# A scan and gated-MLP kernel on one core: VectorE's hand-written order with two weight pieces in turn, and the ninth unit on split weights

## The chip, the cores and the metric

The kernel runs on one core of a Trainium2 chip. The metric is the device time of one execution in microseconds, as a median of several runs; lower is better.

## What is computed

The inputs are x (4 batches, 8 heads, 768 positions, 32 values), decays a, and the matrices B and C of a state of 16 values, with three weight matrices of a gated MLP. First a linear attention with decay is computed in chunks, then the MLP on its output, viewed as 3072 tokens of 256 values. The reference, cut to what matters:

```python
for c in range(nc):                                   # chunks of the sequence
    cum = np.cumsum(la, axis=-1)                      # la = log(clip(a, 1e-6, 1))
    L = np.exp(cum[:, :, :, None] - cum[:, :, None, :]) * causal
    M = np.einsum('bhin,bhjn->bhij', Cc, Bc) * L
    y_intra = np.einsum('bhij,bhjd->bhid', M, xc)
    y_inter = np.einsum('bhin,bhnd->bhid', Cc, state) * np.exp(cum)[:, :, :, None]
    y[:, :, sl] = y_intra + y_inter
    state = decay_full[:, :, None, None] * state + np.sum(Bx, axis=2)
g = x @ w_gate                                        # x: y as 3072 x 256; d_ff = 1536
out = (g / (1 + np.exp(-g)) * (x @ w_val)) @ w_out
```

## The kernel before

The sequence is cut into six blocks of 128 positions; a block holds 512 tokens of the four batches together. For each block the kernel scans the decays (L), makes scores (S), mixes them (M), sums states (st) and values (y), and hands x to the MLP. The MLP of a block has twelve units, one for each 128 columns of the 1536: unit f of block k makes a gate half (gv k f 0) and a value half (gv k f 1) in two PSUM banks, ScalarE makes the silu (si k f), VectorE the product (pr k f), and later the output sums (po) follow. Blocks 3 to 5 use a scheme with fewer multiplications, on weight sums that GpSimd makes.

fp32 precision is had in two ways. A whole unit multiplies fp32 weights by fp32 x (four passes a matmul). A split unit uses a high and a low part of both, in three products that run at the faster fp32r rate: xh and xl for x, wh and wl for weights, where the low part is what the rounded high part leaves. The weights come as 64-bit numbers and are converted on the chip, piece by piece (pieces 0 to 11 are the units, 12 to 17 the output weights): mag and rest on ScalarE, range on VectorE or GpSimd, then on VectorE shift, sign and round, each on the result of the one before (lines 704 to 714). round gives the whole weight; wh (ScalarE) and wl follow from it. The first WHOLE units of block 0 (line 1332: nine) run whole, since their high and low parts come later: for these pieces ScalarE writes the negated weight (minus, line 720) and GpSimd starts a DMA that adds the weight to wl (line 729); for later pieces VectorE subtracts (line 732). x's low part in block 0 is made in the same way, by two negated copies on ScalarE (minus x, line 606) and one adding DMA of GpSimd (line 609).

The order of the work is made by a planner when the kernel is built (class Plan, lines 49 to 195): each step has an engine, a cost, a rank, prerequisites and buffers, and the planner issues steps as they come free on its own clock. For the first 60 us the order is instead written out by hand, one list for each engine (FRONT, lines 1346 to 1375). An engine runs its list in this order; a step that waits holds up all behind it. Behind the lists the planner is free. FAR (line 1337) names the pieces whose range goes to GpSimd. PSUM has four banks for units (mm): a unit's half takes the bank of the half two units earlier, when si has read the gate half and pr the value half.

What the change touches: the four lists of FRONT for VectorE, ScalarE and GpSimd (TensorE's stays), w_low, the steps of x in block 0 (lines 1230 to 1234), WHOLE, MINUS, FAR, and the order of loads in SP's queue for the later blocks (line 1315).

Of the kernel before, what the change touches and what calls it, by code (L numbers as in the profile page):

```python
# [23 lines left out]
K = P // Q  # L24
# [192 lines left out]
def scan_moe_kernel(ctx: ExitStack, tc, aj, an, bc, xb, wgv, wo, cst, own, first_e, e_table, out):  # L217
# [387 lines left out]

    def first_minus(g):
        se.activation(xl[0][:, g], whole[0][:, g], AF.Copy, scale=-1.0)

    def first_low():
        ge.dma_start(xl[0], whole[0], accum_op=ALU.add)  # L610

# [431 lines left out]
    for i in range(NW):  # L1043
# [7 lines left out]
        e, c = ("Pool", 2.2) if far else ("DVE", 0.335)  # L1051
        add(e, c, do(w_range, i, ge if far else ve), r - 4.5, [("mag", i), *([("round", i - 1)] if i == 1 else [])], gives=("range", i))
        add("Act", 0.57, do(w_rest, i, "Act"), r - 4.5, [("raw", i), *([("xf", 5)] if i == 3 else [])], gives=("rest", i))
# [6 lines left out]
        n, c = (slice(2 * P, 4 * P), 0.35) if not i else (slice(0, 4 * P), 0.6)  # L1060
        add("DVE", 0.335 if i else 0.2, do(w_shift, i, n), r - 4.2, [("range", i), *gate], gives=("shift", i))
        add("DVE", c, do(w_sign, i, n), r - 3.9, [("shift", i), *gate], gives=("sign", i))
        add("DVE", c, do(w_round, i, n), r - 3.3, [("sign", i), ("rest", i)], uses=[("raw", i)], gives=("round", i))
# [76 lines left out]
    for k in range(NB):  # L1140
# [86 lines left out]
        if not k:  # L1227
            add("-", 0.0, new_whole, -9, [("clip", 1)], takes=[("xl", "xf")], gives="xf")
            add("-", 0.0, do(new_x, 0), due(0, WHOLE) - 9, [("xf", i) for i in range(6)], takes=[("xh", ("xh", 0)), ("xl", ("xl", 0))], gives=("x", 0))
            for g in range(2):  # L1230
                r = due(0, WHOLE) - 7 + 2 * g
                add("Act", 0.57, do(first_high, g, "Act"), r, [("x", 0)], gives=("xh", 0, g))
                add("Act", 0.57, do(first_minus, g), r + 0.5, [("x", 0), ("gv", 0, 4, 0)], gives=("minus", "x", g))
            add("Pool", 1.2, first_low, due(0, WHOLE) - 4.5, [("minus", "x", g) for g in range(2)], uses=["xf"], gives=("xl", 0, 0), lag=1.6)
            for n, i in enumerate(FIRST_X):
                add([("Act", 0.2 if i % 3 else 0.36)], None, do(x_whole, i), -1 + n / 10, [("y" if i % 3 else "vals", *((0,) if i % 3 else ()), i // 3), "xf"], uses=[y[i]], gives=("xf", i))
            continue
# [9 lines left out]
    for k in range(FAST):  # L1247
        xs = [(t, k, i) for t in ("xh", "xl") for i in range(2 * K if k else 2) if k or t == "xh" or not i]
        for f in range(NF):
# [63 lines left out]
    for steps in ORDER:  # L1313
        plan.follow(steps)
    for k in range(FAST + 1, NB):
        plan.follow([("aj", k), ("bc", k), ("E", k), ("xb", k)])
# [31 lines left out]
clip 0, clip 1, row, scan0 0, scan0 1, scan0 2, scan0 3, L 0 0, L 0 1, L 0 2, L 0 3, bt 0, M 0 0, M 0 1, ce 0, M 0 2, M 0 3,  # L1348
shift 0 gate, sign 0 gate, round 0 gate, shift 0, sign 0, round 0, range 1, shift 1, sign 1, round 1, range 2, products, shift 2, sign 2, round 2,
pr 0 0, shift 3, sign 3, round 3, pr 0 1, shift 4, sign 4, round 4, step 0 1, shift 5, pr 0 2, sign 5, round 5,  # L1350
shift 6, sign 6, round 6, pr 0 3, shift 7, sign 7, round 7, shift 8, sign 8, pr 0 4, round 8, L 1 0, L 1 1, L 1 2, pr 0 5,
L 1 3, shift 9, bt 1, sign 9, M 1 0, pr 0 6, M 1 1, M 1 2, M 1 3, round 9, pr 0 7, wl 9, shift 10, sign 10, round 10,
pr 0 8, wl 10, ce 1, step 1 0, shift 11, sign 11, round 11, pr 0 9, wl 11, pr 0 10, xh 1 0, xh 1 2, xl 1 0, xl 1 2, xl 1 1, xl 1 3,
step 1 1, shift 12, pr 0 11, sign 12, round 12, wl 12
# [87 lines left out]
```

## Time and profile before

| What | Before |
|---|---|
| Median of 3 runs | 339.32 us (338.32 to 340.19) |
| Profiled execution | 337.55 us, its span 335.8 us |
| TensorE busy (matmul) | 330.2 us, 98% of the span |
| VectorE, ScalarE, GpSimd busy | 70%, 52%, 54% |
| Mean granted clock of TensorE | 0.998 |

The span runs from the first to the last instruction of the profiled execution. All instructions of the kernel are recorded by one helper and so have one line (L206); they are told apart by the tiles they write and read. wg8w is the weight of piece 8 while it is converted, wg8h and wg8l its high and low part, sg a silu or product, T the states. A shift is a TENSOR_SCALAR on int32, a range one on f32, a sign a SCALAR_TENSOR_TENSOR, a round the CUSTOM instruction. Matmuls overlap one another, so a duration of one is longer than the distance to the next.

### The profile page before, as it was taken

To read this page: it belongs to the slowest core of one execution; us is meant where nothing else is said; L and a number is where in the kernel's file an instruction comes from. 1 tells how busy PE (TensorE), PEld (TensorE's weight loads), DVE (VectorE), ACT (ScalarE), POOL (GpSimd) and SP (SyncE) were. 2 spreads that over 40 slices of the span, in tenths; PEclk is the share of its full clock that TensorE was granted. 3 is DMA by queue.
4 is the path that set the end of the run, shared out by engine and by line. 5 is a ranking of instruction groups with operands and counts; after the bars stand their busy time and mean duration, and the time that the engine had idled before them with its cause. 6 is when DMAs were issued, how large, how long until landed. Compare 5 with 4: busy or idle time off the path is not lost.

```text
span 335.8 us, 8400 instructions
## 1 busy us (share of the span) xinstructions
PE 330.2 (98%) x3506; PEld 276.3 (82%) x3506; DVE 235.0 (70%) x411; ACT 175.0 (52%) x321; POOL 181.3 (54%) x164
## 2 busy tenths in 40 slices
PE   7999999999999999999999999999999999999996
PEld 6645757888888888878888999888999978999985
DVE  7899999878699981575199478843499934376600
ACT  5799957546245543545371686332575341656411
POOL 2378841511213109887979997450479560368460
PEclk9999999999999999999999999999999999999999
DMA  7899975990000761000091100008500000100001
GB/s 249 288 395 284 261 163 152 297 228 15 1 2 8 206 169 63 1 2 2 17 241 62 62 2 2 2 4 217 164 0 1 5 2 2 62 2 0 2 0 62
DMA packets 10100, 31.05 MB, mean 92 GB/s; under 512 B 1455, under 2 KB 2223, under 8 KB 9423
## 3 DMA queue, kind: packets, MB, share of 16 engines
q1 hardware_dynamic: 7192, 24.21, 23.7%
q0 software_dynamic: 1440, 2.88, 4.8%
q10 hardware_dynamic: 1431, 3.43, 3.5%
q8 instruction: 27, 0.44, 0.6%
q14 instruction: 10, 0.08, 0.1%
HBM read 24.29 MB, written 3.35 MB: 82 GB/s over the span
## 4 chain that ended last, share of the span: by engine, by line
PE 95%; DVE 2%; DMA 1%; issue 0%; SPq 0%; DVEq 0%
PE po L206 30%; PE gv L206 29%; PE pq L206 23%; PE y L206 5%; PE r L206 4%; PE S L206 2%; DVE L L206 1%; PE a L206 1%; DMA pick<-in_own 1%; DVE sg L206 0%; PE st L206 0%; DVE wg9w L206 0%; DVE wg8w L206 0%; PE rest L206 0%; DVE last L206 0%
## 5 line engine op out<-in xcount | busy, mean ns | idle before, releaser
L206 POOL TENSOR_TENSOR pl<-hp,ph 128x512 fp32r<-128x512 f32 x36 | 46.7, 1310 | 25.8 <-PE po L206 14.9
L206 POOL TENSOR_TENSOR sp<-sp 128x256 f32<-128x256 f32 x36 | 30.5, 848 | 32.0 <-ACT sp L206 29.9
L206 DVE TENSOR_TENSOR pq<-pq,sp 128x512 f32<-128x512 f32 x36 | 25.0, 694 | 14.4 <-PE pq L206 14.3
L206 ACT COPY sp<-pq 128x512 f32<-128x512 f32 x36 | 21.1, 587 | 20.2 <-PE pq L206 19.8
L206 ACT ACTIVATE sg<-gv 128x512 f32<-128x512 f32 x36 | 21.5, 597 | 17.6 <-PE gv L206 17.3
L206 DVE TENSOR_TENSOR_SCAN L<-L,dj 128x520 f32<-128x520 f32 x20 | 29.5, 1506 | 0.9 <-DMA L<-clipped 0.9
L206 DVE TENSOR_TENSOR sp<-r,sp 128x256 f32<-128x256 f32 x36 | 15.0, 418 | 20.4 <-POOL sp L206 20.4
L206 DVE TENSOR_TENSOR sg<-gv,sg 128x512 f32<-128x512 f32 x28 | 19.2, 684 | 11.5 <-PE gv L206 8.8
L206 ACT ACTIVATE hp<-pq 128x512 f32<-128x512 f32 x36 | 20.2, 602 | 11.0 <-DVE pq L206 9.6
L206 ACT CAST ph<-hp 128x1024 fp32r<-128x1024 f32 x18 | 18.8, 1052 | 13.1 <-PE po L206 7.9
L206 ACT COPY ob<-po 128x512 f32<-128x512 f32 x12 | 7.0, 587 | 35.4 <-PE po L206 34.9
L206 DVE TENSOR_TENSOR hp<-pq,hp 128x512 f32<-128x512 f32 x36 | 23.6, 684 | 2.0 <-PE pq L206 1.4
L206 ACT CAST hh<-sg 128x512 fp32r<-128x512 f32 x23 | 14.3, 620 | 13.7 <-PE po L206 9.7
L206 DVE TENSOR_TENSOR hh<-sg,hh 128x512 fp32r<-128x512 f32 x28 | 20.7, 762 | 0.8 <-ACT hh L206 0.7
L206 DVE TENSOR_TENSOR L<-S,L 128x512 f32<-128x512 f32 x24 | 15.1, 682 | 0.5 <-PE S L206 0.5
L206 DVE TENSOR_TENSOR gv<-gv,sg 128x512 f32<-128x512 f32 x8 | 5.6, 700 | 10.8 <-PE gv L206 10.8
L206 PEld LDWEIGHTS y<-L,xb 64*32 64x32 f32 x768 | 9.2, 110 | 2.9 <-issue 1.1
L206 PE MATMUL y<-L,xb 64*32 64x64 f32 x768 | 11.4, 233 | 0.0
L206 POOL TENSOR_TENSOR wdl<-wd,wdh 128x512 fp32r<-128x512 f32 x6 | 8.2, 1366 | 4.3 <-ACT wdh L206 4.3
L206 DVE TENSOR_TENSOR last<-po,ob 128x256 f32<-128x256 f32 x1 | 0.4, 424 | 13.7 <-PE po L206 13.7
L206 POOL TENSOR_TENSOR wt<-wg0h,wg0l 128x512 f32<-128x512 f32 x1 | 1.3, 1285 | 16.1 <-DVE xb L206 16.1
L206 ACT CAST hh<-gv 128x512 fp32r<-128x512 f32 x8 | 4.7, 587 | 9.7 <-DVE gv L206 9.7
(675 smaller groups left out, 1124.9 us busy)
## 6 DMA issues: line engine op xcount, KB each, us to landing
L<-clipped SPq DMA_DIRECT2D x10, 520.0 KB, 9.7
xb<-in_xb SPq DMA_DIRECT2D x6, 768.0 KB, 13.3
bc<-in_bc SPq DMA_DIRECT2D x6, 512.0 KB, 6.6
out<-ob SPq DMA_DIRECT2D x11, 256.0 KB, 5.0
E<-clipped SPq DMA_DIRECT2D x5, 260.0 KB
wg0r<-in_wgv SPq DMA_DIRECT2D x1, 512.0 KB
wg1r<-in_wgv SPq DMA_DIRECT2D x1, 512.0 KB, 6.3
wg2r<-in_wgv SPq DMA_DIRECT2D x1, 512.0 KB
```

Of the source, the lines that this page charges most:

```text
L206: ins = getattr(self.engine, name)(*a, **k)
```

## The change

All edits are in one file. WHOLE goes from 9 to 8, so the ninth unit of block 0 runs on split weights, and its wl is made by a subtraction on VectorE. x's low parts in block 0 are made by two subtractions on VectorE (xl 0 0, xl 0 1). Ranges 3 and 9 go to VectorE and range 2 to GpSimd. VectorE's list is rewritten so that steps of two weight pieces, or of a piece and something else, take turns; products, round 9, M 1 1, M 1 2 and step 0 1 change places. ScalarE's list loses the negated copies, and wh 8 and wh 9 move ahead of wh 5, and wh 10 ahead of mag 12. Three prerequisites of the planner are dropped. From block 3 on, the loads of a block are put in the order decays (aj), bc, E, xb; before, this held from block 4 on.

```diff
+    def first_low(g):
+        ve.tensor_tensor(out=xl[0][:, g], in0=whole[0][:, g], in1=xh[0][:, g].bitcast(F32), op=ALU.subtract)
...
-        add(e, c, do(w_range, i, ge if far else ve), r - 4.5, [("mag", i), *([("round", i - 1)] if i == 1 else [])], gives=("range", i))
+        add(e, c, do(w_range, i, ge if far else ve), r - 4.5, [("mag", i)], gives=("range", i))
...
-        add("DVE", 0.335 if i else 0.2, do(w_shift, i, n), r - 4.2, [("range", i), *gate], gives=("shift", i))
-        add("DVE", c, do(w_sign, i, n), r - 3.9, [("shift", i), *gate], gives=("sign", i))
+        add("DVE", 0.335 if i else 0.2, do(w_shift, i, n), r - 4.2, [("range", i)], gives=("shift", i))
+        add("DVE", c, do(w_sign, i, n), r - 3.9, [("shift", i)], gives=("sign", i))
...
-                add("Act", 0.57, do(first_minus, g), r + 0.5, [("x", 0), ("gv", 0, 4, 0)], gives=("minus", "x", g))
-            add("Pool", 1.2, first_low, due(0, WHOLE) - 4.5, [("minus", "x", g) for g in range(2)], uses=["xf"], gives=("xl", 0, 0), lag=1.6)
+                add("DVE", 0.6, do(first_low, g), r + 0.5, [("xh", 0, g)], uses=["xf"], gives=("xl", 0, g))
...
-    for k in range(FAST + 1, NB):
+    for k in range(FAST, NB):
         plan.follow([("aj", k), ("bc", k), ("E", k), ("xb", k)])
...
-WHOLE = 9
+WHOLE = 8
...
-FAR = [0, *range(3, 18)]
+FAR = [0, 2, *range(4, 9), *range(10, 18)]
...
     DVE="""
-shift 0 gate, sign 0 gate, round 0 gate, shift 0, sign 0, round 0, range 1, shift 1, sign 1, round 1, range 2, products, shift 2, sign 2, round 2,
-pr 0 0, shift 3, sign 3, round 3, pr 0 1, shift 4, sign 4, round 4, step 0 1, shift 5, pr 0 2, sign 5, round 5,
-shift 6, sign 6, round 6, pr 0 3, shift 7, sign 7, round 7, shift 8, sign 8, pr 0 4, round 8, L 1 0, L 1 1, L 1 2, pr 0 5,
-L 1 3, shift 9, bt 1, sign 9, M 1 0, pr 0 6, M 1 1, M 1 2, M 1 3, round 9, pr 0 7, wl 9, shift 10, sign 10, round 10,
-pr 0 8, wl 10, ce 1, step 1 0, shift 11, sign 11, round 11, pr 0 9, wl 11, pr 0 10, xh 1 0, xh 1 2, xl 1 0, xl 1 2, xl 1 1, xl 1 3,
+shift 0 gate, sign 0 gate, shift 0, round 0 gate, sign 0, round 0, range 1, shift 1, sign 1, products, round 1, shift 2, sign 2, range 3, round 2,
+shift 3, pr 0 0, sign 3, shift 4, round 3, pr 0 1, sign 4, shift 5, round 4, sign 5, shift 6, pr 0 2, round 5,
+sign 6, shift 7, round 6, pr 0 3, sign 7, xl 0 0, round 7, xl 0 1, shift 8, pr 0 4, sign 8, range 9, round 8, shift 9, L 1 0, sign 9, L 1 1, round 9, pr 0 5, L 1 2,
+wl 8, L 1 3, bt 1, M 1 0, M 1 1, M 1 2, pr 0 6, M 1 3, shift 10, pr 0 7, sign 10, wl 9, round 10, step 0 1, pr 0 8,
+shift 11, wl 10, ce 1, sign 11, step 1 0, round 11, pr 0 9, wl 11, pr 0 10, xh 1 0, xh 1 2, xl 1 0, xl 1 2, xl 1 1, xl 1 3,
...
     Act="""
-rest 8, xh 0 1, wh 0, minus 0, si 0 4, minus x 0, minus x 1, mag 9, rest 9, wh 1, minus 1, wh 2, minus 2, wh 3, si 0 5, raw 12, wh 4,
-mag 10, rest 10, wh 5, wh 6, wh 7, wh 8, si 0 6, raw 13, mag 11, si 0 7, rest 11, minus 3, minus 4, wh 9,
-si 0 8, mag 12, rest 12, rest 13, minus 5, wh 10, ap 1 0, ap 1 1, si 0 9, raw 14, wh 11, si 0 10, raw 15, minus 6, minus 7,
+rest 8, xh 0 1, wh 0, minus 0, si 0 4, mag 9, rest 9, wh 1, minus 1, wh 2, minus 2, wh 3, si 0 5, raw 12, wh 4,
+mag 10, rest 10, wh 8, wh 9, wh 5, wh 6, wh 7, si 0 6, raw 13, mag 11, si 0 7, rest 11, minus 3, minus 4, si 0 8,
+wh 10, mag 12, rest 12, rest 13, minus 5, ap 1 0, ap 1 1, si 0 9, raw 14, wh 11, si 0 10, raw 15, minus 6, minus 7,
...
     Pool="""
-e rest, e low, clipped, range 0, range 3, range 4, range 5, range 6, range 7, range 8, wl 0, range 9, xl 0 0, wl 1, range 10, wl 2, wl 3, range 11,
-wl 4, wl 5, wl 6, range 12, wl 7, wl 8, range 13
+e rest, e low, clipped, range 0, range 2, range 4, range 5, range 6, range 7, range 8, wl 0, wl 1, range 10, wl 2, wl 3, range 11,
+wl 4, wl 5, wl 6, range 12, wl 7, range 13
```

## Rows read from the trace of the kernel before

**Rows 1.** The page: busy us of each engine (share, instructions); the chain by engine

```profile
PE 330.2 (98%) x3506; PEld 276.3 (82%) x3506; DVE 235.0 (70%) x411; ACT 175.0 (52%) x321; POOL 181.3 (54%) x164
PE 95%; DVE 2%; DMA 1%; issue 0%; SPq 0%; DVEq 0%
```

**Rows 2.** The chain that ended last, in order of time: start us, us, what

```profile
37.65 3.79 DVE L L206 x3
...
45.20 0.69 DVE sg L206
...
45.93 1.98 PE gv L206 x4
...
130.08 16.32 PE gv L206 x72
146.40 1.14 PE S L206 x63
```

**Rows 3.** Waits of TensorE, whole span: us in total, times, longest us

```profile
PE gv L206 <- DVE sg L206: 0.2, 1, 0.2
```

**Rows 4.** Timeline of TensorE: start us, us, instructions [idle before]

```profile
21.90 3.60 PE L206 MATMUL gv<-xf,wg2w 128*128 128x512 f32 x8
25.33 3.60 PE L206 MATMUL gv<-xf,wg3w 128*128 128x512 f32 x8
...
43.89 1.88 PE L206 MATMUL gv<-xf,wg8w 128*128 128x512 f32 x4
...
52.20 0.74 PE L206 MATMUL gv<-xh,wg10h 128*128 128x512 f32 x2
```

**Rows 5.** Timeline of VectorE, 16 to 50 us

```profile
16.72 0.69 DVE L206 SCALAR_TENSOR_TENSOR wg1w<-wg1r,wg1w 128x512 int32<-128x512 int32 x1
17.55 0.70 DVE L206 CUSTOM_DVE_ANT_0 wg1w<-wg1r,wg1w 128x1024 uint16<-128x1024 uint16 x1
...
18.96 0.77 DVE L206 TENSOR_SCALAR wg2w<-wg2w 128x512 int32<-128x512 int32 x1
...
26.87 1.22 DVE L206 SCALAR_TENSOR_TENSOR T<-T,E 128x64 f32<-128x64 f32 x4
28.01 0.42 DVE L206 TENSOR_SCALAR wg5w<-wg5w 128x512 int32<-128x512 int32 x1
28.35 0.68 DVE L206 TENSOR_TENSOR sg<-gv,sg 128x512 f32<-128x512 f32 x1
28.95 1.10 DVE L206 SCALAR_TENSOR_TENSOR wg5w<-wg5r,wg5w 128x512 int32<-128x512 int32 x1
...
30.69 0.42 DVE L206 TENSOR_SCALAR wg6w<-wg6w 128x512 int32<-128x512 int32 x1
31.14 0.69 DVE L206 SCALAR_TENSOR_TENSOR wg6w<-wg6r,wg6w 128x512 int32<-128x512 int32 x1
31.87 0.69 DVE L206 CUSTOM_DVE_ANT_0 wg6w<-wg6r,wg6w 128x1024 uint16<-128x1024 uint16 x1
32.48 0.68 DVE L206 TENSOR_TENSOR sg<-gv,sg 128x512 f32<-128x512 f32 x1
...
48.96 0.69 DVE L206 TENSOR_TENSOR wg9l<-wg9w,wg9h 128x512 fp32r<-128x512 f32 x1
```

**Rows 6.** Timeline of GpSimd: two ranges, the longest and one of the shortest of eight

```profile
20.73 2.33 POOL L206 TENSOR_SCALAR wg4w<-wg4w 128x512 f32<-128x512 f32 x1
...
28.89 1.91 POOL L206 TENSOR_SCALAR wg8w<-wg8w 128x512 f32<-128x512 f32 x1
```

**Rows 7.** Timeline of ScalarE: the magnitude of piece 2, the high part of piece 10

```profile
16.21 0.68 ACT L206 ACTIVATE wg2w<-wg2r 128x512 f32<-128x512 f32 x1
...
51.53 0.61 ACT L206 CAST wg10h<-wg10w 128x512 fp32r<-128x512 f32 x1
```

**Rows 8.** Timelines of SP and VectorE: loads and first scan of the fourth block

```profile
108.84 1.54 SPq L206 DMA_DIRECT2D L<-clipped  x2
...
119.13 1.24 DVE L206 TENSOR_TENSOR_SCAN L<-L,dj 128x520 f32<-128x520 f32 x1 [0.94 <-DMA L<-clipped]
```

More of the change, by code (lines that the diff above doesn't have):

```diff
@@ L604, in first_high @@
         copy(e, xh[0][:, g], whole[0][:, g])
[L606 to L610, printed above, removed]
+    def first_low(g):
+        ve.tensor_tensor(out=xl[0][:, g], in0=whole[0][:, g], in1=xh[0][:, g].bitcast(F32), op=ALU.subtract)
     def x_low(k, i):
@@ L1247, in scan_moe_kernel @@
     for k in range(FAST):
-        xs = [(t, k, i) for t in ("xh", "xl") for i in range(2 * K if k else 2) if k or t == "xh" or not i]
+        xs = [(t, k, i) for t in ("xh", "xl") for i in range(2 * K if k else 2)]
         for f in range(NF):
@@ L1331 @@
 LATER = 3.0
-WHOLE = 9
+WHOLE = 8
 HALVED = 5, 6
 LAST = (5, 6, 9, 10, 11, 12)
-MINUS = (3, 3, 4, 5, 5, 5, 10, 10, 10)
+MINUS = (3, 3, 4, 5, 5, 5, 10, 10)
 FEW = 8
-FAR = [0, *range(3, 18)]
+FAR = [0, 2, *range(4, 9), *range(10, 18)]
 PAGE = 4.4
@@ L1358 @@
 mag 3, rest 3, mag 4, rest 4, si 0 1, mag 5, rest 5, written e, mag 6, rest 6, xh 0 0, si 0 2, mag 7, rest 7, Cz 1, si 0 3, mag 8,
-rest 8, xh 0 1, wh 0, minus 0, si 0 4, minus x 0, minus x 1, mag 9, rest 9, wh 1, minus 1, wh 2, minus 2, wh 3, si 0 5, raw 12, wh 4,
-mag 10, rest 10, wh 5, wh 6, wh 7, wh 8, si 0 6, raw 13, mag 11, si 0 7, rest 11, minus 3, minus 4, wh 9,
-si 0 8, mag 12, rest 12, rest 13, minus 5, wh 10, ap 1 0, ap 1 1, si 0 9, raw 14, wh 11, si 0 10, raw 15, minus 6, minus 7,
-xh 1 1, xh 1 3, minus 8, rest 14, si 0 11, raw 16, si 1 0, wh 12, si 1 1, mag 13, raw 17, hh 0 0, si 1 2, hh 0 2, rest 15,
+rest 8, xh 0 1, wh 0, minus 0, si 0 4, mag 9, rest 9, wh 1, minus 1, wh 2, minus 2, wh 3, si 0 5, raw 12, wh 4,
+mag 10, rest 10, wh 8, wh 9, wh 5, wh 6, wh 7, si 0 6, raw 13, mag 11, si 0 7, rest 11, minus 3, minus 4, si 0 8,
+wh 10, mag 12, rest 12, rest 13, minus 5, ap 1 0, ap 1 1, si 0 9, raw 14, wh 11, si 0 10, raw 15, minus 6, minus 7,
+xh 1 1, xh 1 3, rest 14, si 0 11, raw 16, si 1 0, wh 12, si 1 1, mag 13, raw 17, hh 0 0, si 1 2, hh 0 2, rest 15,
 si 1 3, wh 13, si 1 4, mag 14, rest 16, si 1 5, rest 17, si 1 6, Cz 2
```

## The prediction

> **What bounds the kernel now.** I read the page first, for its busy shares and its chain. TensorE is busy for 98% of the span and is 95% of the chain that ended last [rows 1]: this kernel is a queue of matmuls, and time can be won only by taking matmul work out or by closing gaps between matmuls. Then I read the waits of TensorE over the whole span. Behind the start of the kernel there is a single one over 0.15 us, on a product of VectorE [rows 3]. The chain in order of time says where: from 36.96 us it leaves TensorE and runs through VectorE's scans of the second block, up to the product that ends at 45.88, and only then back to TensorE [rows 2]. That product is pr 0 6. It empties the PSUM bank of the seventh unit's value half, and with four such banks used in turn it is the bank that gv 0 8 1, the second half of the ninth unit, writes. The first half began at 43.89 [rows 4], and its four matmuls take 4 x 0.43 = 1.72 us, so TensorE was free at 45.61 and went on at 45.93. So in the first block two engines are nearly level: TensorE sets the time, and VectorE, which has no idle time over 0.15 us between 16 and 60 us, is 0.3 us behind it. All steps of the change are in that stage, apart from one, and the question is which of the two it makes longer.
>
> **Part 1, the ninth unit on split weights.** Taken from TensorE: a plain fp32 unit takes 25.33 - 21.90 = 3.43 us [rows 4], a split one of twelve matmuls 12 x 16.32 / 72 = 2.72 us [rows 2]. That is 0.71 us, all of it on the path, half of it in gv 0 8 0 and half in gv 0 8 1. Added on VectorE: wl 8, one subtraction. Its neighbour wl 9 lasts 0.69 us [rows 5]; a two-input instruction of this size lets the next one start after 0.61 us where it depends on nothing just before it (31.87 to 32.48) [rows 5]. Taken from ScalarE and GpSimd: one negated copy and one adding DMA, neither on the path.
>
> **Part 2, x's low parts by VectorE.** Two subtractions, 2 x 0.61 = 1.22 us more on VectorE. What goes is two negated copies on ScalarE and one DMA issue of GpSimd, whose result was needed by the tenth unit at 49 us; nobody waited for it, so this earns nothing.
>
> **Part 3, ranges.** Ranges 3 and 9 move from GpSimd to VectorE, 2 x 0.34 us (28.01 to 28.35 is the pitch of such an instruction with a stranger behind it) [rows 5]; range 2 goes the other way. This adds a wait: shift 2 now waits for GpSimd. The magnitude of piece 2 is done at 16.21 + 0.68 = 16.89 [rows 7], a range takes GpSimd 1.91 to 2.33 us [rows 6], so shift 2 starts between 18.9 and 19.4; I take 19.25, against 18.96 before [rows 5]: 0.29 us later. Behind it on VectorE stands the whole chain to pr 0 6. TensorE does not feel it directly: gv 0 2 starts after 22 us and round 2 is done before.
>
> **Part 4, alternation.** A piece needs shift, sign and round, each on the result of the one before. Side by side, shift to sign takes 0.45 us (30.69 to 31.14) and sign to round 0.73 (31.14 to 31.87), for pieces 1 to 3 even 0.83 (16.72 to 17.55) [rows 5]. With another piece's step in between the pitches are 0.34 and 0.61. Between shift 2 and pr 0 6 the old order has five side-by-side pairs of the first kind, 5 x 0.11 = 0.55 us, and six of the second, 2 x 0.22 + 4 x 0.12 = 0.92. The new order has only shift 2 and sign 2 left, which it had before too. Saved: 1.47 us.
>
> The Trainium skill speaks against this part: "VectorE: DVE Perf Modes", section "The DRAIN you can't avoid", says that a semaphore between chained instructions costs nothing extra, because the pipe drains either way. By that the 1.47 us would be 0. The trace disagrees here, with 0.73 against 0.61 us behind the same instruction [rows 5].
>
> **Part 5, what stands ahead of pr 0 6.** In the new list round 9 and M 1 1 and M 1 2 stand ahead of it, 3 x 0.61 = 1.83 us, and step 0 1 behind it; that occupied 26.87 to 28.01, 1.14 us, of which 0.35 is a collision as in part 6, so 0.79 [rows 5]. products moves ahead of round 1, which takes round 1 from 0.83 behind its sign to about 0.61 + 0.47, 0.24 us later (0.6, if GpSimd's range 2 collides with it). gv 0 1 followed round 1 at once before, so all of TensorE's units move by 0.24 to 0.6 us; I take 0.4.
>
> **Part 6, collisions.** In the stretch from 18.96 to 45.20 GpSimd runs eight ranges (3 to 10). During seven of them one VectorE instruction is 0.35 to 0.41 us longer than its like: the 28.95 instruction takes 1.10 us where the same form takes 0.69, beginning as GpSimd's range 8 begins at 28.89 [rows 5, 6]. They sum to 2.63 us, 0.33 for each range. In the new order six ranges lie in the stretch (4 to 8 and 10): 1.97 us, 0.66 less. From both sides: 0, if all fall on products, which read PSUM and were not hit, and 6 x 0.41 = 2.46, and one more hit of 0.41 if range 11 falls there.
>
> **The sum.** pr 0 6 moves by 0.29 (part 3) + 0.68 (two ranges) + 6 x 0.61 (two low parts of x, wl 8, round 9, two M) - 0.79 (step 0 1) - 1.47 (alternation) - 0.66 (collisions) = +1.71 us, from 45.20 to 46.91. TensorE would reach gv 0 8 1 at 43.89 + 0.4 + 1.36 + 0.1 (its restart) = 45.75, and gets the bank at 46.91 + 0.68 + 0.05 = 47.64: it now waits 1.9 us, where it waited 0.3. gv 0 8 1 starts 1.71 us later and is 0.35 shorter, so the work behind it starts 1.36 later. Then one small gap closes: gv 0 10 started at 52.20, just behind wh 10, which ended at 51.53 + 0.61 [rows 4, 7]; TensorE comes later now, and about 0.2 us of gap and restart go. Net +1.1 to 1.2 us; I take +1.1. Behind that no wait of TensorE is left [rows 3], so nothing absorbs it and nothing adds.
>
> Two more waits are put in, both on ScalarE. wh 9 stands ahead of wh 5, 6, 7 and si 0 6; round 9 ends near 41.0, four casts of some 0.52 and the silu bring si 0 6 to 43.8, and it frees the bank of gv 0 8 0, wanted at 44.3: 0.5 us of cover. The load raw 13 is issued behind it, near 44; its first user, rest 13, stands behind wh 10 and comes near 52. wh 10 stands ahead of four copies and ap 1 0, for which step 1 0 and then y 1 wait; by the same count step 1 0 ends near 55.4 and TensorE reaches y 1 near 56.3: 0.9 us.
>
> **Edits with one answer**: the dropped prerequisites (round 0 for range 1, the gate half for shift 0 and sign 0) are the planner's alone; shift 0 between sign 0 gate and round 0 gate fills a gap ahead of a step that waits for ScalarE anyway; the constants only set ranks. Nothing.
>
> **The fourth block's loads**: its decays now go ahead of bc 3 in SP's queue. SP spends 1.54 us on issuing them, and VectorE's first scan waited 0.94 us for them at 119.13 [rows 8]. That wait may go and bc 3 comes some 1.5 us later; TensorE begins that block's scores only at 146.40 [rows 2], so I cost this at nothing, covered by some 20 us.
>
> The profiled execution took 337.55 us around a span of 335.8; the median of the runs is 339.32 (338.32 to 340.19). The sum gives 338.65 for the profiled one, and 340.4 as a median.
>
> **Rivals.**
> A, VectorE is on time. If the collisions go to 0 and GpSimd's range 2 takes 1.91 us, pr 0 6 starts near 44.6 and its bank is free before 45.6. TensorE then keeps the 0.71 us and the 0.3 us of its old wait, pays 0.24 for products, and gains the 0.2 at gv 0 10: about -1.0 us, 338.3. The old order's seven hits in eight speak against it. The kernel is no slower than before if pr 0 6 starts 1.1 us earlier than in my sum; no wait is left at 1.9 us earlier.
> B, the collisions come in full. Seven hits of 0.41 and a range 2 of 2.33 us put pr 0 6 at 47.9: +2.2 us, 341.5. Slower than before by a measurable amount from pr 0 6 at 47.5.
> C, alternation saves nothing, because each step drains anyway: the 1.47 us come back and the sum is +2.6 us, 341.9. The pitches of 0.61 against 0.73 speak against it [rows 5]. It is the Trainium skill's rule named in part 4.
> D, the steps behind the fixed lists are ordered anew. The planner sets their order itself from changed costs; a step that feeds TensorE may come too late in one of the later switches between units and attention. TensorE has no gap there now, so this can only cost: one more wait like the present one and up to some 3 us, 340 to 343.
>
> **How the numbers follow.** My forecast 0.50 (+0.3 to +1.7 us), A 0.24 (from -1.0 up to +0.3), B 0.14, C 0.04, D 0.08. A measurement of this kernel tells about 0.5%, 1.7 us, from no change. No more than about 1.9 us can be won at all: 0.71 of matmuls and 1.2 of gaps that are not restarts; so faster gets 0.05, out of A. Slower is B, C and D, 0.26; the same 0.69. The range goes from A's 338.3, less 0.3 us for the spread of runs, to C's 341.9: 338.0 to 342.0.
>
> **What would show it.** In the profile after: a wait of gv for VectorE's product near 46 to 47.6 us of 1 to 2.5 us (forecast, B) or none (A); pr 0 6 starting near 46.9; sign to round pitches of 0.61 plus what stands between (against C); shift 2 behind a range 2 of GpSimd at 19.25; twelve matmuls for the ninth unit at 0.227 us; TensorE without waits behind 60 us (against D). It is wrong if VectorE's steps are hit less often, or if a wait that I covered, si 0 6 or ap 1 0, becomes the last.

## The result

| | Before | Changed |
|---|---|---|
| Median | 338.17 us (6 runs) | 342.44 us (6 runs, 340.53 to 344.66) |
| Profiled execution, its span | 337.55 us, 335.8 us | 344.66 us, 342.9 us |
| A second profile of the changed kernel | | 341.99 us, 340.2 us |
| TensorE busy, mean granted clock | 330.2 us, 0.998 | 333.0 us, 0.995 |

The changed kernel takes 1.0123 times the time of before, with a 95% interval of 1.0074 to 1.0173: it is slower, by 4.3 us. The forecast was +1.1 us with a range up to 342.0, so the time lies 0.4 us above the range.

The page of the profile after, busy time of each engine and the chain by engine, to be laid beside [rows 1]:

```profile
PE 333.0 (97%) x3510; PEld 279.0 (81%) x3510; DVE 235.8 (69%) x413; ACT 174.7 (51%) x320; POOL 176.4 (51%) x161
PE 83%; DMA 7%; DVE 7%; issue 2%; POOL 1%; ACT 1%; DVEq 0%
```

TensorE's share of the chain falls from 95% to 83%, and VectorE and DMA have 7% each. TensorE has one unit less of plain fp32 and is nevertheless 2.8 us longer busy. Most of that belongs to the start of this one execution, where the first unit took 5.56 us instead of 3.70; in the second profile TensorE is busy for 330.2 us, as before: there what the split unit saves stands against what a lower clock costs behind the first wait below. Two rows of TensorE's waits over the whole span (us in total, times, longest us); the profile before has nothing of the first and 0.2 us of the second [rows 3]:

```profile
PE y L206 <- DVE T L206: 2.2, 1, 2.2
PE gv L206 <- DVE sg L206: 1.0, 1, 1.0
```

The second row is the wait that was forecast, on pr 0 6. The first is one that was not: y 1 waits for the states T, which step 1 0 makes. Who is late there is seen in VectorE's timeline of the same profile (start us, us, instruction, idle time before it and what ended it):

```profile
54.00 0.86 DVE L206 SCALAR_TENSOR_TENSOR T<-T,E 128x64 f32<-128x64 f32 x4
...
58.84 0.69 DVE L206 TENSOR_TENSOR bc<-bc,E 128x512 f32<-128x512 f32 x1 [2.44 <-DMA E<-clipped]
59.45 0.69 DVE L206 SCALAR_TENSOR_TENSOR wg11w<-wg11r,wg11w 128x512 int32<-128x512 int32 x1
60.05 0.85 DVE L206 SCALAR_TENSOR_TENSOR T<-T,E,y 128x64 f32<-128x64 f32 x4
```

and in SP's queue, first of before, then of after:

```profile
31.06 0.67 SPq L206 DMA_DIRECT2D E<-clipped  x1
```

```profile
54.89 0.66 SPq L206 DMA_DIRECT2D E<-clipped  x1
```

The first row of VectorE is step 0 1. It reads the first block's E, and E has one buffer. The change moves this step from 26.87 us [rows 5] to 54.00, and SP can only then issue the load that overwrites E, at 54.89 instead of 31.06. ce 1 (bc<-bc,E) waits 2.44 us for that load, step 1 0 stands behind ce 1, and y 1 behind step 1 0. The issue is a row of 0.66 us; ce 1 begins 3.95 us after it began. The Trainium skill ("Perfetto Trace Analysis", section "Per-instruction lifecycle: what the profiler-reported window actually captures") says that the row of a DMA instruction leaves the data movement out, and the trace agrees: the load has to be looked for in the wait of its first reader.

What comes behind that wait is seen in the windows of the same profile (stretch; its length; busy us and instructions of PE, PEld, DVE, ACT, POOL; then PEclk, DMA share, GB/s):

```profile
56.00:58.00 2.00, 2.00 (x10) 1.66 (x9) 0.40 (x1) 1.94 (x6) 0.75 (x1) 1.00 0.41 118
58.00:61.00 3.00, 0.85 (x4) 0.38 (x2) 2.16 (x7) 0.68 (x2) 0.10 (x1) 1.00 0.75 162
61.00:65.00 4.00, 3.96 (x132) 3.39 (x133) 3.92 (x9) 3.27 (x7) 1.54 (x2) 0.57 0.92 266
65.00:70.00 5.00, 5.00 (x23) 4.13 (x22) 3.82 (x11) 1.82 (x3) 2.15 (x2) 1.00 1.00 307
```

The granted clock is 1.00 up to the wait, 0.57 on average in the four microseconds behind it (0.5, that is 1.2 GHz, for most of them) and 1.00 again afterwards. TensorE pays for the wait twice.

### The profile page after: what moved, and what is told of

Its sections match the earlier page's. It is cut to its first block, busy times and chain, and to the rows that moved or that the text cites. A ratio compares the mean times of both kernels' runs of the same rounds, so it can differ in the third digit from the quotient of the medians.

```text
span 342.9 us, 8400 instructions
## 1 busy us (share of the span) xinstructions
PE 333.0 (97%) x3510; PEld 279.0 (81%) x3510; DVE 235.8 (69%) x413; ACT 174.7 (51%) x320; POOL 176.4 (51%) x161
## 3 DMA queue, kind: packets, MB, share of 16 engines
q10 hardware_dynamic: 1431, 3.43, 3.7%
## 4 chain that ended last, share of the span: by engine, by line
PE 83%; DMA 7%; DVE 7%; issue 2%; POOL 1%; ACT 1%; DVEq 0%
PE po L206 29%; PE pq L206 23%; PE gv L206 20%; PE y L206 5%; PE r L206 4%; DMA wg11r<-in_wgv 3%; DMA xb<-in_xb 2%; DVE L L206 2%; PE S L206 1%; DMA E<-clipped 1%; DVE sg L206 1%; DVE wg3w L206 1%; DVE wg9w L206 1%; DVE wg10w L206 1%; POOL wg2w L206 1%
## 5 line engine op out<-in xcount | busy, mean ns | idle before, releaser
L206 ACT COPY sp<-pq 128x512 f32<-128x512 f32 x36 | 21.1, 587 | 20.5 <-PE pq L206 20.1
L206 PE MATMUL y<-L,xb 64*32 64x64 f32 x768 | 12.1, 245 | 0.7 <-issue 0.7
L206 POOL TENSOR_TENSOR wt<-wg0h,wg0l 128x512 f32<-128x512 f32 x1 | 1.3, 1287 | 20.5 <-DVE xb L206 20.5
```

What stands on the lines that cost most here:

```text
L206: ins = getattr(self.engine, name)(*a, **k)
```

## The ledger of the changed kernel

The first profile of the changed kernel began its first unit 2.1 us late and ran half of it at half the pace (0.85 us a matmul instead of 0.43). No clock is on record for these matmuls: the trace's record of the granted clock begins at 20.5 us, with 1.00, just where the pace doubles. The second profile, of the same kernel, has neither, so that belongs to the run and not to the change. From TensorE's timelines of before and of the second profile, the starts in us:

| Start of | Before | Changed | Later by |
|---|---|---|---|
| gv 0 0 | 14.65 | 14.36 | -0.29 |
| gv 0 1 | 18.39 | 18.59 | +0.20 |
| gv 0 7 | 40.44 | 40.64 | +0.20 |
| gv 0 9 | 49.27 | 50.08 | +0.81 |
| y 1 | 55.18 | 58.28 | +3.10 |
| gv 0 11 | 56.81 | 60.37 | +3.56 |
| S of the third block | 92.41 | 96.91 | +4.50 |
| span | 335.8 | 340.2 | +4.4 |

Its TensorE timeline around the two waits:

```profile
18.59 3.67 PE L206 MATMUL gv<-xf,wg1w 128*128 128x512 f32 x8 [0.56 <-DVE wg1w L206]
...
47.08 0.73 PE L206 MATMUL gv<-xh,wg8h 128*128 128x512 f32 x2 [1.46 <-DVE sg L206]
...
58.28 1.04 PE L206 MATMUL y<-bc,T 32*64 32x64 f32 x64 [2.43 <-DVE T L206]
59.25 1.19 PE L206 MATMUL y<-L,xb 64*32 64x64 f32 x64
60.37 1.22 PE L206 MATMUL gv<-xh,wg11h 128*128 128x512 f32 x2
```

From gv 0 0 to gv 0 9 the changed kernel loses 0.81 + 0.29 = 1.10 us: that is the loss that was forecast, in its place (the sum had 1.36 us here and took 0.2 off again at the next unit). The wait of y 1 adds 3.10 - 0.81 = 2.29 us, and the half clock behind it 4.50 - 3.10 = 1.40 us (y 1 takes 2.09 us instead of 1.63, gv 0 11 the rest). Behind that the shift stays between +4.4 and +4.5 to the end. So 3.7 of 4.4 us come from something that the forecast did not contain.

The other executions bear the price of the clock out. Nine of the ten on record of the changed kernel have a mean granted clock of 0.995 or less over the whole run and a median of 342.3 us; the tenth, at 1.000, took 340.53 us, the least of all.

## Experiments

T1 is the theory that the late step 0 1 costs through E's only buffer, with the clock behind it. T2 is the forecast's own cause, VectorE's longer list ahead of pr 0 6, as the whole of the loss. The medians, all beside runs of before on the same chip:

| Run | Median us | Before us | Ratio, 95% interval |
|---|---|---|---|
| e0_after | 342.14 | 337.55 | 1.0126 (1.0079 to 1.0173) |
| e1_step_back | 339.98 | 337.55 | 1.0064 (1.0036 to 1.0092) |
| e2_step_late | 344.16 | 337.55 | 1.0188 (1.0134 to 1.0241) |
| e3_turns | 337.21 | 337.55 | 0.9989 (0.9960 to 1.0018) |
| e4_unit_alone | 339.00 | 337.44 | 1.0026 (0.9997 to 1.0055) |
| e5_two_E | 338.34 | 337.44 | 1.0020 (0.9995 to 1.0045) |
| e6_product_early | 338.75 | 337.44 | 1.0034 (1.0008 to 1.0060) |
| e7_both | 337.29 | 337.44 | 0.9990 (0.9971 to 1.0009) |
| e8_two_E_early | 337.89 | 337.34 | 0.9999 (0.9968 to 1.0030) |
| e9_step_back_early | 337.76 | 337.34 | 1.0008 (0.9982 to 1.0035) |
| e10_sums_early | 337.83 | 337.45 | 1.0018 (0.9998 to 1.0038) |
| e11_low_by_dma | 336.69 | 337.45 | 0.9988 (0.9966 to 1.0009) |

### The changed kernel once more

> The changed kernel once more, unaltered, for its profile. In its first profile the first value unit (gv 0 0) ran four matmuls at half clock (5.56 us instead of 3.70) and everything behind began 3.7 us later than before. If that belongs to the run, gv 0 1 begins here near 18.4 to 19 us and the profiled time is near 341; if it belongs to the change, it is near 22 us again. Theory T1 (the late load of E) expects in either case the same wait of y 1 for VectorE, 2.0 to 2.4 us, and a stretch at granted clock 0.5 behind it. Time 340.5 to 344.5.

gv 0 1 began at 18.59 and the time was 342.14: the late start was the run's. (The half clock that the expectation names for the first unit is read from the pace, as said above.) The wait of y 1 (2.43 us) and the half clock behind it came again. This is the profile of the ledger above.

### Step 0 1 back in its place

```diff
-shift 3, pr 0 0, sign 3, shift 4, round 3, pr 0 1, sign 4, shift 5, round 4, sign 5, shift 6, pr 0 2, round 5,
+shift 3, pr 0 0, sign 3, shift 4, round 3, pr 0 1, sign 4, shift 5, round 4, step 0 1, sign 5, shift 6, pr 0 2, round 5,
...
-... sign 10, wl 9, round 10, step 0 1, pr 0 8,
+... sign 10, wl 9, round 10, pr 0 8,
```

> The changed kernel with one step moved: step 0 1 stands behind round 4 again, as before, instead of behind round 10. T1 (step 0 1 is the last reader of the only buffer of E, SP's load of the next E waits for it, and y 1 waits for what follows): the load is issued near 31 us again instead of 55, the wait of y 1 (2.2 us) and the half clock behind it (1.3 us) go, 3 to 3.5 us faster than the changed kernel, 337.5 to 339.5, about level with before. T2 (it is VectorE's longer list ahead of pr 0 6, as forecast, that costs the time): step 0 1 adds 0.8 us ahead of pr 0 6, so 0 to 0.8 us slower than the changed kernel, 342 to 343.5, and TensorE's wait for pr 0 6 grows from 1.0 to about 1.8 us.

339.98 us, 2.2 us faster than the changed kernel and 0.5 us above the range that T1 gave; by the profiled spans it is 2.8 us faster (337.4 against 340.2). In the profile the load of E is issued at 31.53 us, y 1 waits for nothing and the clock is 1.000. Four of the twelve executions have a mean clock of 0.995 and took 339.7 to 341.0 us; the profiled one took 339.14. The longest row among TensorE's waits is now

```profile
PE gv L206 <- DVE sg L206: 2.2, 1, 2.2
```

T1 gave the direction and T2 the size of what is left: step 0 1 now stands ahead of pr 0 6 again, and the wait for pr 0 6 grows by 2.20 - 1.46 = 0.74 us, as the forecast's 0.79 us for this step has it. The 3.7 us are gone in this profile, and some of them are paid back here.

### Step 0 1 late in the kernel before

```diff
-pr 0 0, shift 3, sign 3, round 3, pr 0 1, shift 4, sign 4, round 4, step 0 1, shift 5, ...
+pr 0 0, shift 3, sign 3, round 3, pr 0 1, shift 4, sign 4, round 4, shift 5, ...
...
-... round 9, pr 0 7, wl 9, shift 10, sign 10, round 10,
+... round 9, pr 0 7, wl 9, shift 10, sign 10, round 10, step 0 1,
```

> The kernel before with only step 0 1 moved, from behind round 4 to behind round 10. T1: the load of the next E is issued near 50 us instead of 31, ce 1 waits for it, y 1 waits some 2 us for VectorE and the clock falls behind it: 2 to 3.5 us slower than before, 340.5 to 342. T2: pr 0 6 comes 0.8 us earlier, the 0.3 us wait for it goes, 0.3 to 0.4 us faster than before, 337.5 to 338.

344.16 us, 6.6 us slower than before, with this one step moved: T1's direction, and twice the 2 to 3.5 us that it expected. The load is issued at 51.40 us. ce 1 and y 1 in VectorE's timeline and in TensorE's waits:

```profile
57.37 0.69 DVE L206 TENSOR_TENSOR bc<-bc,E 128x512 f32<-128x512 f32 x1 [4.80 <-DMA E<-clipped]
```

```profile
PE y L206 <- DVE T L206: 4.0, 1, 4.0
```

Here ce 1 begins 5.97 us after the issue instead of some 4, and behind the longer wait the shift against before grows from 3.80 us at y 1 to 5.85 at the third block's S: 2.05 us for the clock. pr 0 6 did come 0.85 us earlier (44.35), as T2 says, and from gv 0 8 to gv 0 9 that won 0.4 us (4.94 instead of 5.38); the wait of y 1 swallowed them.

### Two buffers for E

```diff
-    att.tile([P, 24], F32, name="gap2")
+    att.tile([P, 16], F32, name="gap2")
...
-        bl[k]["E"] = att.tile([P, BATCH, K, W], F32, tag="E", name=f"E{k}")
+        bl[k]["E"] = att.tile([P, BATCH, K, W], F32, tag="E", name=f"E{k}", bufs=2)
```

To make room for the second buffer, an unused gap tile is cut by 32 bytes in each partition. The hand-written lists stay.

> The changed kernel with the same lists, step 0 1 late as it is there, but two buffers for E. T1 says that step 0 1 costs only through the buffer: the load of the next E no longer waits for it and is issued near 31 us, ce 1 waits for no DMA, y 1's wait (2.4 us) and the half clock behind it (1.4 us) go: 3.5 to 3.9 us faster than the changed kernel, 338.3 to 339, which is the sum that was forecast (+0.8 to +1.1 us). Rival: the place of step 0 1 on VectorE itself delays y 1 (it stands shortly ahead of step 1 0, which y 1 needs); then two buffers change nothing and the time stays at 342.

338.34 us: 3.8 us faster than the changed kernel and 0.9 us slower than before. Step 0 1 is as late as in the changed kernel (51.95 us), but the load is issued at 33.03, ce 1 begins without a wait, and y 1 too. What is left of TensorE's waits is the one for pr 0 6 that was forecast and 0.7 us for round 1; the two rows between belong to the start of the kernel:

```profile
PE gv L206 <- DVE sg L206: 1.4, 1, 1.4
PE rest L206 <- DVE warm L206: 1.1, 1, 1.1
PE a L206 <- DVE rows L206: 1.0, 1, 1.0
PE gv L206 <- DVE wg1w L206: 0.7, 1, 0.7
```

This separates the cause: not the place of step 0 1 on VectorE, but the buffer that it holds. It also shows what the forecast's sum was worth: without the step that it overlooked, the change costs 0.9 us where +1.1 was forecast (the interval is -0.2 to +1.5 us).

### What is left: pr 0 6 earlier

```diff
-wl 8, L 1 3, bt 1, M 1 0, M 1 1, M 1 2, pr 0 6, M 1 3, shift 10, ...
+wl 8, L 1 3, bt 1, M 1 0, pr 0 6, M 1 1, M 1 2, M 1 3, shift 10, ...
```

This is on top of e1_step_back.

> The kernel of run e1_step_back with M 1 1 and M 1 2 behind pr 0 6 instead of ahead of it. If VectorE's work ahead of pr 0 6 is what is left of the loss there (a wait of 2.2 us of gv 0 8 1), pr 0 6 begins 1.2 us earlier, near 46.3, the wait falls to 1.0 us, and the time to 338.6 to 339, 1.0 to 1.2 us faster than e1_step_back. Rival: what is left comes from later (the switches behind 60 us) or from the clock; then 339.5 to 340 as there.

338.75 us, as expected, and 1.2 us under the median of e1_step_back, though the two intervals overlap. pr 0 6 begins at 46.49 instead of 47.54 us, and the wait for it is 0.99 us. So VectorE's work ahead of pr 0 6 is what that wait was made of; that it is what was left of the time isn't shown. In the profile gv 0 9 begins 1.0 us earlier than in e1_step_back, but behind it TensorE waits 0.38 us for wl 9 and 0.23 us for step 1 0:

```profile
51.86 0.73 PE L206 MATMUL gv<-xh,wg9l 128*128 128x512 f32 x2 [0.38 <-DVE wg9l L206]
```

So y 1 begins at 56.92 where it began at 56.96. The spans are 337.2 and 337.4 us: the wait moved on. What else the medians differ by is open; none of the twelve executions here has a mean clock under 0.998, four there have 0.995.

### Alternation alone

```diff
-... round 0, range 1, shift 1, sign 1, round 1, range 2, products, shift 2, sign 2, round 2,
-pr 0 0, shift 3, sign 3, round 3, pr 0 1, shift 4, sign 4, round 4, step 0 1, shift 5, pr 0 2, sign 5, round 5,
-shift 6, sign 6, round 6, pr 0 3, shift 7, sign 7, round 7, shift 8, sign 8, pr 0 4, round 8, ...
+... round 0, range 1, shift 1, range 2, sign 1, shift 2, round 1, sign 2, products, round 2,
+shift 3, pr 0 0, sign 3, pr 0 1, round 3, shift 4, step 0 1, sign 4, shift 5, round 4, pr 0 2, sign 5, shift 6, round 5,
+sign 6, shift 7, round 6, pr 0 3, sign 7, shift 8, round 7, sign 8, pr 0 4, round 8, ...
```

> The kernel before with only VectorE's list changed so that steps of pieces 1 to 8 take turns with steps of other pieces; step 0 1 stays early (one place earlier), WHOLE, ranges, x's low parts and the other lists stay. By the pitches of the trace (0.60 in turns, 0.73 to 0.83 side by side) pr 0 6 begins 1.2 to 1.5 us earlier than 45.2, the 0.3 us wait for it goes: 0.3 to 0.6 us faster, 337.5 to 338. By the rule of the Trainium skill (VectorE: DVE Perf Modes, section on the DRAIN) that a semaphore costs nothing beside the drain, pr 0 6 begins at 45.2 as before and nothing changes.

pr 0 6 begins at 42.51 us, 2.7 us earlier than before, more than expected (GpSimd's ranges hit fewer steps as well), and the time is the same. TensorE's wait for pr 0 6 is gone, but round 1, with two steps of others ahead of it, is late:

```profile
PE gv L206 <- DVE wg1w L206: 0.7, 1, 0.7
```

So alternation does free VectorE, and TensorE was on time but for 0.3 us: there was nothing to give it to. In VectorE's timeline the steps stand 0.60 us apart in turns, for instance

```profile
27.52 0.68 DVE L206 SCALAR_TENSOR_TENSOR wg5w<-wg5r,wg5w 128x512 int32<-128x512 int32 x1
28.12 0.42 DVE L206 TENSOR_SCALAR wg6w<-wg6w 128x512 int32<-128x512 int32 x1
28.46 0.68 DVE L206 CUSTOM_DVE_ANT_0 wg5w<-wg5r,wg5w 128x1024 uint16<-128x1024 uint16 x1
29.06 0.68 DVE L206 SCALAR_TENSOR_TENSOR wg6w<-wg6r,wg6w 128x512 int32<-128x512 int32 x1
```

against 0.73 side by side [rows 5]. The rule of the Trainium skill that was weighed in the prediction, that a semaphore costs nothing beside the drain, is not borne out by these rows.

### The split unit alone, and both together

```diff
-WHOLE = 9
+WHOLE = 8
...
-L 1 3, shift 9, bt 1, sign 9, M 1 0, pr 0 6, ...
+L 1 3, wl 8, shift 9, bt 1, sign 9, M 1 0, pr 0 6, ...
...
-mag 10, rest 10, wh 5, wh 6, wh 7, wh 8, si 0 6, ...
+mag 10, rest 10, wh 8, wh 5, wh 6, wh 7, si 0 6, ...
```

(The negated copy and the adding DMA of piece 8 go too.)

> The kernel before with the ninth unit on split weights alone: WHOLE 8, wl 8 by a subtraction of VectorE behind L 1 3, wh 8 two casts earlier; the rest of VectorE's order side by side as before, x's low part by the adding DMA as before. By the sum: TensorE saves 0.71 us, pr 0 6 begins 0.6 us later (45.8), gv 0 8 1 waits 1.1 us for it instead of 0.3: +0.1 to +0.4 us, 337.6 to 338. By the matmuls alone: 0.7 us faster, 336.8.

339.00 us, by the medians 1.6 us slower than before, with an interval that still holds 1; the sum said +0.1 to +0.4. In the profile pr 0 6 came at 47.29, not at 45.8: the units began 0.36 us later in this execution, and sign 9 ahead of pr 0 6 took 1.80 us instead of 0.68. Whether the other executions were hit in the same way no trace shows; six of the twelve have a mean clock of 0.995. The row of sign 9, and GpSimd's at that time:

```profile
44.97 1.80 DVE L206 SCALAR_TENSOR_TENSOR wg9w<-wg9r,wg9w 128x512 int32<-128x512 int32 x1
```

```profile
44.70 0.86 POOL L206 DMA_DIRECT2D wg3l<-wg3w  x1 [2.96 <-ACT wg3l L206]
45.28 2.25 POOL L206 TENSOR_SCALAR wg11w<-wg11w 128x512 f32<-128x512 f32 x1
```

e7_both is e3_turns with this edit, and with round 1 straight behind sign 1 again.

> The kernel before with the two parts together: the alternating order of e3_turns, with the head as before (round 1 straight behind sign 1, so that gv 0 1 doesn't wait), and the split ninth unit of e4_unit_alone. Step 0 1 early, the ranges and x's low part as before. pr 0 6 begins near 43.5 us, its bank is free near 44.2, TensorE wants it near 45.3: no wait. The matmuls' 0.71 us and the old wait of 0.3 us with its restart are both earned: 1.1 to 1.4 us faster than before, 336.1 to 336.5. Rival: something else becomes the last (wh 8 or wl 8 late for gv 0 8, wl 9 late for the tenth unit): 337 to 337.5.

337.29 us, level with before: the rival came true, by two things at once. x's low part by the adding DMA comes too late for the ninth unit, and VectorE was hit like that again (round 7, 1.87 us), so that pr 0 6 began at 45.95 us instead of near 43.5. TensorE's timeline, VectorE's, and the DMA's time from issue to landing:

```profile
45.85 0.73 PE L206 MATMUL gv<-xl,wg8h 128*128 128x512 f32 x2 [0.78 <-DMA xl<-xf]
```

```profile
34.13 1.87 DVE L206 CUSTOM_DVE_ANT_0 wg7w<-wg7r,wg7w 128x1024 uint16<-128x1024 uint16 x1
```

```profile
xl<-xf POOLq DMA_DIRECT2D x1, 512.0 KB, 9.4
```

For part 2 of the prediction, that moving x's low part to VectorE "earns nothing", this has to be read beside e4_unit_alone, where the ninth unit is split too and the DMA is as before. There it was issued at 35.23 us and took 8.7 us, so it landed some 0.8 us ahead of its first reader, and nobody waited:

```profile
35.23 0.95 POOL L206 DMA_DIRECT2D xl<-xf  x1
```

```profile
44.72 0.62 PE L206 MATMUL gv<-xl,wg8h 128*128 128x512 f32 x2
```

In e7_both it was issued 1.2 us later, behind two ranges of GpSimd that took 3.34 and 3.48 us instead of some 2:

```profile
30.27 3.48 POOL L206 TENSOR_SCALAR wg8w<-wg8w 128x512 f32<-128x512 f32 x1
...
36.39 1.24 POOL L206 DMA_DIRECT2D xl<-xf  x1
```

So the split ninth unit alone doesn't make the DMA late; together with the alternation on VectorE it was 0.8 us late. e3_turns, which has the alternation too, has a range of 3.43 us. Why the ranges are longer there was not tested.

### A version without the late steps

e8_two_E_early is e5_two_E with round 1 ahead of products, M 1 1, M 1 2 and round 9 behind pr 0 6, and wl 9 ahead of sign 10 (on ScalarE wh 9 goes back behind minus 4):

```diff
-... shift 1, sign 1, products, round 1, shift 2, ...
+... shift 1, sign 1, round 1, products, shift 2, ...
...
-... L 1 1, round 9, pr 0 5, L 1 2,
-wl 8, L 1 3, bt 1, M 1 0, M 1 1, M 1 2, pr 0 6, M 1 3, shift 10, pr 0 7, sign 10, wl 9, round 10, ...
+... L 1 1, pr 0 5, L 1 2,
+wl 8, L 1 3, bt 1, M 1 0, pr 0 6, M 1 1, M 1 2, M 1 3, round 9, pr 0 7, shift 10, wl 9, sign 10, round 10, ...
```

> The kernel of run e5_two_E with VectorE's steps for TensorE earlier: round 1 straight behind sign 1 and products behind it, M 1 1, M 1 2 and round 9 behind pr 0 6 (so wh 9 goes back behind minus 4 on ScalarE), wl 9 ahead of sign 10. If VectorE ahead of the second block's attention is all that is left, gv 0 1 no longer waits 0.7 us, pr 0 6 begins 1.8 us earlier (near 45.5 instead of 47.3) and the wait of gv 0 8 1 shrinks from 1.4 us to 0.3; VectorE then ends M 1 3 near 48.0 where TensorE wants it near 47.9. 1.0 to 1.5 us faster than e5_two_E: 336.8 to 337.4, 0 to 0.6 us faster than before. Rival: the wait moves on to wl 9 or M 1 3 behind pr 0 6 and the time stays at 338.

e9_step_back_early is the same with one buffer of E and step 0 1 behind round 4.

> The same with one buffer for E and step 0 1 early instead (behind round 4, 0.8 to 1.1 us of VectorE ahead of pr 0 6). pr 0 6 begins near 46.5, gv 0 8 1 waits about 1.3 us: 0.7 to 1.1 us slower than e8_two_E_early, 337.7 to 338.3, still 1.5 to 2 us faster than e1_step_back. If step 0 1 fits in a place where VectorE is not the last, the two are level.

337.89 and 337.76 us, the two level, and level with before. e8's 336.8 to 337.4 us are missed; its rival, that the wait moves on, came true. In e8 the wait for pr 0 6 is gone and 0.47 us of wait for wl 10 have come; in e9, 0.42 us are left at pr 0 6, and y 1 waits again, though for another reason:

```profile
55.89 0.90 PE L206 MATMUL y<-bc,T 32*64 32x64 f32 x64 [0.73 <-DVE T L206]
```

Here step 1 0 had waited 0.75 us for the copy ap 1 0 on ScalarE, which stands behind wh 10 and four copies. e10_sums_early puts it straight behind wh 10:

```diff
-wh 10, mag 12, rest 12, rest 13, minus 5, ap 1 0, ap 1 1, si 0 9, ...
+wh 10, ap 1 0, ap 1 1, mag 12, rest 12, rest 13, minus 5, si 0 9, ...
```

> Run e9_step_back_early with ap 1 0 and ap 1 1 (the copies of the block sums, for which step 1 0 and then y 1 wait) straight behind wh 10 on ScalarE, ahead of the magnitude and rests of the output weights. There y 1 waited 0.7 us for step 1 0, and step 1 0 had waited 0.75 us for that copy. If ScalarE's order is the cause, the wait goes: 0.6 to 0.8 us faster than e9_step_back_early, 337.0 to 337.2. If VectorE is late there anyway, no change.

337.83 us, no faster. The wait of y 1 did go, and the third block's S begins 0.60 us earlier than before. The gain is lost far behind it: the fourth block's S begins only 0.4 us earlier than before, at 145.96, and at the end the two are level. TensorE now waits for ScalarE in the fourth block's units, near 191 us,

```profile
PE pq L206 <- ACT hp L206: 0.2, 1, 0.2
```

and that is the only wait over 0.15 us there; the rest of the loss is not traced to a cause. The span is 335.8 us as before. It looks like rival D of the prediction in small, but no run tests that.

e11_low_by_dma takes x's low part off VectorE once more, with the negated copies and the DMA of before put early:

```diff
-... sign 7, xl 0 0, round 7, xl 0 1, shift 8, ...
+... sign 7, round 7, shift 8, ...
...
-... mag 7, rest 7, Cz 1, si 0 3, ...
+... mag 7, rest 7, minus x 0, minus x 1, Cz 1, si 0 3, ...
...
-... range 7, range 8, wl 0, wl 1, ...
+... range 7, xl 0 0, range 8, wl 0, wl 1, ...
```

> Run e10_sums_early with x's low parts made as in the kernel before (two negated copies on ScalarE, one adding DMA of GpSimd), but early: the copies behind rest 7, the DMA ahead of range 8, so that it lands well before the ninth unit needs it (in e7_both, issued at 36.4 us, it landed at 45.8, 0.8 us too late). VectorE loses two subtractions of 0.60 us ahead of pr 0 6; its 0.4 us wait and the start of the second block's sums (st) behind M 1 3 no longer hold TensorE: 0.4 to 0.8 us faster than e10_sums_early, 336.3 to 336.8, and so faster than before by 0.5 to 1.0 us. Rival: GpSimd's issue of the DMA holds a step of VectorE by 1.1 us, as it did once in e4_unit_alone and once in e7_both, and nothing is won.

336.69 us, 0.8 us under the median of before and the fastest of all; its interval still holds 1. The DMA is issued at 28.11 us and needs 10.6 us, in time by far. A step of VectorE was held in this run too (round 5, 1.41 us instead of 0.68, as GpSimd issued the DMA and began range 8), as the rival has it, but less than the 1.1 us feared. Behind two rows of the start, the longest waits of TensorE are

```profile
PE y L206 <- issue: 0.3, 1, 0.3
PE gv L206 <- DVE sg L206: 0.2, 1, 0.2
PE y L206 <- DVE L L206: 0.2, 1, 0.2
```

The two rows of y belong to the start as well. So the parts of the change, with step 0 1 early and VectorE's list shorter, come to some 0.8 us by the medians, which these runs do not tell from nothing.

## Why the prediction was wrong

**The step that failed** is in part 5: "step 0 1 behind it; that occupied 26.87 to 28.01 ... so 0.79". The move was costed as VectorE time alone, as a gain. Step 0 1 is also the last reader of E's only buffer; the load behind it in SP's queue, ce 1, step 1 0 and y 1 form a chain of their own. Nothing of this showed as a wait in the profile of before, where the load was issued at 31.06 us and ce 1 began at 52.78: there were some 18 us of cover, and the move took 24 to 27 us. The planner did not see it either, since the step is entered there without E among the buffers that it uses. This gave +2.3 us in the second profile, and with the clock behind it 3.7; that it is the step is shown by e2_step_late (the step alone), that it is the buffer by e5_two_E (the buffer alone).

**The clock** was no term of the sum. The wait of y 1 was not forecast, and so its price, 1.40 us more at 1.2 GHz, was not either.

**The miss is larger than the 0.4 us** by which the time lies above the range. The forecast stood on a median of before of 339.32 us from three runs; with six it is 338.17, and 337.3 to 337.6 in the series beside the experiments. The change itself was forecast at +1.1 us and measured at +4.3.

**Without the missed step the sum held**: e5_two_E, where that step costs nothing, is 0.9 us slower than before against +1.1 (the interval is -0.2 to +1.5). Its main terms came near one by one, as follows, so this is no luck.

**Part 1 (split unit)**: right. From gv 0 7 to gv 0 9 the shift grows by 0.61 us in the second profile; with the unit's 0.71 us saved and the old wait of 0.17 gone, a wait of 1.46 makes 1.46 - 0.17 - 0.71 = 0.58. (The prediction's old wait of 0.3 us is 0.17 in the profile; the rest is TensorE's restart.)

**Part 2 (x's low parts)**: its price is right (the two take 1.2 us in all). That it earns nothing holds in e4_unit_alone, by 0.8 us; in e7_both, with the alternation, the DMA was 0.8 us late.

**Part 3 (ranges)**: shift 2 does wait for GpSimd, 0.34 us, and begins at 18.78, where 19.25 was forecast; the first unit began 0.29 us earlier than before in this profile. Range 2 took 2.21 us, inside the 1.91 to 2.33 us of [rows 6], which are not the whole spread: range 10 took 2.79 us before.

**Part 4 (alternation)**: pitches of 0.60 us between the long steps in turn; rival C fell.

**Part 5, products**: the units were to move by 0.4 us; gv 0 1 waited 0.56 and moved by 0.49 against its own start.

**Part 6 (collisions)**: forecast 1.97 us between shift 2 and pr 0 6. VectorE's timeline of the second profile has five steps there that are 0.36 to 0.41 us longer, 1.95 us in all; two of the five met the same range, so the sum fits better than the picture of one for each range. Two of them, and pr 0 6:

```profile
26.17 1.09 DVE L206 SCALAR_TENSOR_TENSOR wg5w<-wg5r,wg5w 128x512 int32<-128x512 int32 x1
...
37.64 1.05 DVE L206 SCALAR_TENSOR_TENSOR wg9w<-wg9r,wg9w 128x512 int32<-128x512 int32 x1
...
46.35 0.68 DVE L206 TENSOR_TENSOR sg<-gv,sg 128x512 f32<-128x512 f32 x1
```

The last row is pr 0 6, at 46.35 us where 46.91 was forecast, and 0.47 us of the difference are there already at shift 2; the wait for it is 1.46 and not 1.9 us.

**The covers on ScalarE**: si 0 6 held. For ap 1 0 the 0.9 us of cover were too much: where y 1 does not wait for E, step 1 0 waits some 0.75 us for this copy (e1, e6, e9), and y 1 itself not measurably (under 0.15 us) in e1, 0.23 us in e6 and 0.73 us in e9.

**The fourth block's loads** cost nothing, as said; the first scan still waited 1.19 us for them in the second profile, and no TensorE wait followed.

**Rivals.** A fell (pr 0 6 came late), B and C too. D's 340 to 343 us hold the measured time, but by luck: D is an order that the planner sets anew behind the lists, and the late step stands in a list. Only e10 shows a loss in D's place.

## What to carry to other kernels

A step that is moved takes its buffers along: before a move is priced, ask of each tile that it reads whether it is the last reader, who refills the tile, and who reads the refill, even where the profile shows no wait on that chain. A cover of 18 us is not seen in any row of waits and has to be worked out from the issue and the first reader. And freeing an engine that is not the last gains nothing by itself: alternation gave VectorE 2.7 us (some of it from fewer hits by GpSimd) and the kernel none that could be told from noise.

## What the runs showed of the hardware

A wait of TensorE of 2.2 to 4.0 us at y 1 came with granted clock 0.5 in all three profiles that had it: for some 3 us behind the wait in the two of the changed kernel, and for some 7 us in e2_step_late, where it began while TensorE still waited. A wait of 2.2 us ten microseconds earlier, for pr 0 6, left the clock at 1.00 in the profiles of e1_step_back and e4_unit_alone. The windows of e1_step_back:

```profile
46.00:48.00 2.00, 0.08 (x1) 0.00 (x0) 2.00 (x4) 1.44 (x3) 1.26 (x2) 1.00 0.00 0
48.00:50.00 2.00, 1.73 (x23) 1.19 (x31) 2.00 (x4) 0.00 (x0) 2.00 (x2) 1.00 0.77 131
```

But these two profiles are not the whole record. Each other execution has a mean clock on record: 0.995 in four of twelve of e1_step_back and in six of twelve of e4_unit_alone, against 0.994 in one of twelve of e5_two_E, where that wait is 1.4 us, and 0.990 to 0.995 in four of 58 executions of before beside them. So the earlier wait seems to cost clock too, in some executions; where in them the slow stretch lies, no trace shows. What decides wasn't tried and stays open. The price behind y 1 is 1.3 to 2.05 us.

While GpSimd ran its ranges, single steps of VectorE were mostly 0.3 to 0.4 us longer, in the profile of before as in the others; the products, which read PSUM, were not, in the first 60 us of any profile. Larger ones stand where GpSimd also issued an adding DMA: 0.7 us for shift 10 in e0, e1, e3, e5 and e6, behind pr 0 6 and so outside part 6 (the row is e0's):

```profile
47.55 1.12 DVE L206 TENSOR_SCALAR wg10w<-wg10w 128x512 int32<-128x512 int32 x1
```

It is 0.7 us for round 5 in e11, and 1.1 to 1.2 us in e4 and e7; in these three a range began right behind the DMA's issue. That the pair is the cause was not tested, and it isn't enough by itself: before has the same pair at 44.34 and 44.91 us and e3 at 44.86 and 45.43, beside steps of ordinary length.
